# Weight loads cut into twelve pieces and a reordered attention-out chain in a one-core transformer block

## The chip, the cores and the metric

The kernel runs on one core of one Trainium2 chip. The metric is the device time of one execution in microseconds; the median over runs is quoted, and lower is better. The kernel before takes 227.86 us (median of three runs, 227.57 to 228.95). "Same" means within 2%.

Times inside a profile are microseconds from the start of its span. A span is 1.7 to 1.8 us shorter than the time of the same run (229.42 us with a span of 227.7 before).

## The reference

One block on x of shape [1, 2048, 448] in bf16, without biases or learned norms:

```python
phi = lambda t: jnp.where(t > 0, t + 1, jnp.exp(t)) + 1e-6
# A: linear attention, 16 heads of 28
pq, pk = phi(q), phi(k)                       # q, k, v from layernorm(x) @ wqkv
kv  = jnp.einsum("bhsd,bhse->bhde", pk, v)    # sums over ALL 2048 tokens
z   = jnp.einsum("bhsd->bhd", pk)
num = jnp.einsum("bhqd,bhde->bhqe", pq, kv)
den = jnp.einsum("bhqd,bhd->bhq", pq, z)[..., None] + 1e-6
h   = x + (num / den merged over heads) @ wo
# B: GeGLU, hidden width 1792
n   = layernorm(h)
h2  = h + (gelu_tanh(n @ w_gate) * (n @ w_up)) @ w_down
```

What matters: kv and z need every token, so there is a hard boundary. No attention output exists before the last of 16 token tiles (128 tokens each) has gone into kv, and the MLP of a tile needs that tile's attention output. Three MLP weights of 1,568 KB each must be on chip by then.

One thing about correctness: with weights of these scales the MLP's output is tiny beside h (an estimate from the reference's scales puts it below the rounding of h in bf16). So "correct" here vouches for the attention half, hardly for the MLP.

## The kernel before: the parts that matter

The kernel is a task graph. Every task names its engine, the buffers it reads and writes, a rough duration and a *key* (its rank; lower goes first). A list scheduler places the tasks on each engine in the order of its own model of time; the chip then runs these fixed orders, with semaphores for the dependences. The scheduler knows two modes of TensorE, 128 rows (everything except gate and up) and 64 rows (gate in partitions 0 to 63 and up in 64 to 127, side by side: in the trace of before the first gate and the first up matmul both start at 85.04 us). The choice of mode:

```python
if e == "pe":
    cur = [t for t in av if t.mode == pe_mode]
    oth = [t for t in av if t.mode != pe_mode]
    if cur and oth:
        rc = min(max(f, t.ready) for t in cur)
        ro = min(max(f, t.ready) for t in oth)
        hyst = MODE_HYST_64 if pe_mode == 64 else MODE_HYST_128
        av = cur if rc <= ro + hyst else oth      # stays in its mode while it has work
```

Stage 1 normalises x and transposes it. The first four tiles are transposed on TensorE, the other twelve by DMA, issued from SyncE ("SPq" in the profile):

```python
# ... for each tile t: statistics, rstd, xn = normalised x ...
if t < N_PE_TR:        # 4
    # four TensorE transposes, evicted by VectorE
else:
    G.add("sp", lambda e: e.dma_start_transpose(xnT[:, :, tok], xn[:, sl, :]),
          name="xT%d" % t, key=t - 3.0, ...)
```

For each pair of tiles, TensorE then forms K and V from xnT, ScalarE takes exp of K ("ek") and copies V, GpSimd and VectorE finish phi, and TensorE accumulates kv ("acc"). The three MLP weights are one load each, issued from ScalarE's queue ("ACTq") once the last tile of x is there:

```python
big = [b_x[15]]
dma(wgu_sb[0:64, :, :],   B_w_gate.rearrange("(k p) n -> p k n", p=64),  [b_wg], "dwg", ..., q="act", key=8.0, r=big)
dma(wgu_sb[64:128, :, :], B_w_up.rearrange("(k p) n -> p k n", p=64),    [b_wu], "dwu", ..., q="act", key=8.0, r=big)
dma(wd_sb[:, :, :],       B_w_down.rearrange("(j p) n -> p j n", p=128), [b_wd], "dwd", ..., q="act", key=8.0, r=big)
```

The attention-out chain of a tile, `a2_tile(t)`, uses one set of PSUM banks (4, 5, 6) for all tiles:

```python
ka = K_A2 + 0.01 * t if t < 4 else K_Q + 0.04 * (t - 3) + 0.005     # K_A2 = 15.5, K_Q = 17.0
# nd:   psND(bank 4)  = pq^T kvz                           TensorE
# rd, om: o = num * reciprocal(den)                        VectorE
# tro:  transpose o into bank 6 (TensorE), evicted by ScalarE   [t < 2; later tiles by DMA]
# wo:   psH(bank 5)   = o @ wo                             TensorE
# hr:   h = psH + x, statistics, rstd (ScalarE log/exp for t < 2), norm
# trh:  transpose of norm(h) into bank 6 (TensorE), evicted by ScalarE   [t < 2; later by DMA]
```

Its Q groups (16 of them; matmul, exp, clamp, phi) have keys from 17.0. The table of the gelu is preloaded after all exp work. Gate and up then run in chunks of 2, 2, 4, 4, 4 tiles (`gu_chunk`) and down follows tile by tile.

## Time and profile before

The stages, as read from the TensorE timeline ("first K of tile 4" is the first matmul that needs a DMA transpose):

| milestone, us | before |
|---|---|
| first K matmul | 8.18 |
| first K of tile 4 | 31.79 |
| end of the last kv accumulation | 62.53 |
| first gate/up matmul | 85.04 |
| end of span | 227.7 |

The next lines are the profile page of the kernel before, parts 1 and 2: busy time per engine, and the span in 40 slices of 5.7 us. A digit is the busy share in tenths; PEclk is TensorE's granted clock in tenths; the last row is what the DMA engines moved.

```profile
PE 200.5 (88%) x1666; PEld 114.1 (50%) x1666; DVE 124.1 (55%) x320; ACT 75.2 (33%) x193; POOL 54.5 (24%) x121
...
PE   6790039999996769999998999999999999999995
...
PEclk9798556999999779999999999999999999999999
DMA  7969999400001226300166500044520003000011
GB/s 220 322 169 206 213 269 239 94 4 1 0 0 26 46 45 90 60 0 4 46 122 137 96 3 1 3 104 107 105 40 0 3 21 79 23 0 3 1 40 40
```

TensorE is the bound (88%), with a hole in slices 4 to 6 and a weak stretch in slices 13 to 15, each with a lower clock. In the hole the DMA engines are full (9) and move only 206 to 269 GB/s.

The view of stage windows of the kernel before. Columns: window, its length, busy time (and instructions) of the five engines, mean granted clock, DMA share, GB/s.

```profile
8.18:31.79 23.61, 9.36 (x55) 4.14 (x53) 13.03 (x43) 7.46 (x24) 7.81 (x15) 0.72 1.00 210
31.79:62.53 30.74, 30.33 (x185) 15.25 (x186) 12.26 (x24) 13.86 (x30) 14.13 (x25) 0.89 0.42 90
62.53:85.04 22.51, 17.28 (x104) 9.06 (x102) 17.92 (x42) 14.28 (x22) 7.81 (x14) 0.87 0.14 27
85.04:227.70 142.66, 138.83 (x1281) 81.38 (x1280) 76.02 (x197) 37.32 (x113) 22.58 (x52) 1.00 0.22 46
```

In the first window TensorE works 9.4 of 23.6 us; in the third 17.3 of 22.5, part of it at half clock (75.8 to 79.2 us and from 82.6 us on, by the clock records of this trace). The second and the last are nearly full.

The TensorE timeline of the kernel before, around the hole (start, length, instruction, idle time before it and what ended it), and then its table of waits (total, times, longest):

```profile
17.11 0.42 PE L514 MATMUL ps<-v,pk 128*113 128x113 bf16 x4
31.79 1.30 PE L477 MATMUL ps<-wkv_sb,xnT 128*128 128x448 bf16 x3 [14.25 <-DMA xnT<-xn]
33.49 1.30 PE L477 MATMUL ps<-wkv_sb,xnT 128*128 128x448 bf16 x3 [0.41 <-DMA xnT<-xn]
```

```profile
PE ps L477 <- DMA xnT<-xn: 14.7, 2, 14.3
...
PE ps L666 <- DMA hnT<-hn: 1.0, 1, 1.0
```

DMA issues of the kernel before (the last column is the median time from issue to landing), and the view of the xnT tile, which gives that time as minimum, median and maximum over the twelve transposes:

```profile
wgu_sb<-in_B_w_gate_dram ACTq DMA_DIRECT2D x1, 1568.0 KB, 10.4
wgu_sb<-in_B_w_up_dram ACTq DMA_DIRECT2D x1, 1568.0 KB, 17.9
wd_sb<-in_B_w_down_dram ACTq DMA_DIRECT2D x1, 1568.0 KB, 24.3
```

```profile
DMA to landing us min/median/max: 2.4/7.2/17.4
```

A transpose takes 2.4 us when nothing is in its way and up to 17.4 us beside the weights. That is the hole.

ScalarE's timeline of the kernel before, between the last kv accumulation and the first gate/up matmul (other instructions left out), shows four loads of activation tables:

```profile
72.38 1.28 ACT L618 ACT_TABLE_LOAD   x1
...
75.70 1.28 ACT L424 ACT_TABLE_LOAD   x1
...
79.67 1.28 ACT L426 ACT_TABLE_LOAD   x1
...
84.20 1.28 ACT L690 ACT_TABLE_LOAD   x1
```

### The profile page before, as it was taken

To read this page: it belongs to the slowest core of one execution; us is meant where nothing else is said; L and a number is where in the kernel's file an instruction comes from. 1 tells how busy PE (TensorE), PEld (TensorE's weight loads), DVE (VectorE), ACT (ScalarE), POOL (GpSimd) and SP (SyncE) were. 2 spreads that over 40 slices of the span, in tenths; PEclk is the share of its full clock that TensorE was granted. 3 is DMA by queue.
4 is the path that set the end of the run, shared out by engine and by line. 5 is a ranking of instruction groups with operands and counts; after the bars stand their busy time and mean duration, and the time that the engine had idled before them with its cause. 6 is when DMAs were issued, how large, how long until landed. Compare 5 with 4: busy or idle time off the path is not lost.

```text
span 227.7 us, 4477 instructions
## 1 busy us (share of the span) xinstructions
PE 200.5 (88%) x1666; PEld 114.1 (50%) x1666; DVE 124.1 (55%) x320; ACT 75.2 (33%) x193; POOL 54.5 (24%) x121
## 2 busy tenths in 40 slices
PE   6790039999996769999998999999999999999995
PEld 6340004455553338898554555555455554455552
DVE  4988010634599576454877545676654452454422
ACT  3265003465467463344000443300244400344300
POOL 3066024624455036000354100054400030000000
PEclk9798556999999779999999999999999999999999
DMA  7969999400001226300166500044520003000011
GB/s 220 322 169 206 213 269 239 94 4 1 0 0 26 46 45 90 60 0 4 46 122 137 96 3 1 3 104 107 105 40 0 3 21 79 23 0 3 1 40 40
DMA packets 37637, 17.00 MB, mean 75 GB/s; under 512 B 29488, under 2 KB 36720, under 8 KB 37616
## 3 DMA queue, kind: packets, MB, share of 16 engines
q1 hardware_dynamic: 34400, 11.50, 24.0%
q10 hardware_dynamic: 3216, 5.22, 9.6%
q8 instruction: 13, 0.21, 0.4%
q14 instruction: 8, 0.07, 0.1%
HBM read 8.26 MB, written 1.84 MB: 44 GB/s over the span
## 4 chain that ended last, share of the span: by engine, by line
PE 76%; DMA 10%; DVE 8%; ACT 3%; issue 1%; POOL 1%; SPq 0%; DVEq 0%; ACTq 0%
PE ps L666 34%; PE ps L629 18%; DMA xnT<-xn 7%; PE ps L583 5%; PE ps L668 4%; PE ps L485 4%; PE ps L477 4%; PE ps L539 3%; DVE st L414 2%; DVE pqT L544 2%; PE ps L488 2%; PE ps L514 2%; DMA x_sb<-in_A_x_dram 1%; DMA hnT<-hn 1%; DVE x_sb L586 1%
## 5 line engine op out<-in xcount | busy, mean ns | idle before, releaser
L666 PE MATMUL ps<-hnT,wgu_sb 64*128 64x512 bf16 (+1 forms) x490 | 86.0, 335 | 1.0 <-DMA hnT<-hn 1.0
L668 PE MATMUL ps<-hnT,wgu_sb 64*128 64x512 bf16 (+1 forms) x490 | 86.1, 335 | 0.0
L690 ACT ACTIVATE gl<-ps 128x256 bf16<-128x256 f32 x112 | 36.9, 381 | 92.6 <-PE ps L668 57.3
L692 DVE TENSOR_TENSOR hh<-ps,gl 128x256 bf16<-128x256 f32 x112 | 42.3, 420 | 43.0 <-ACT gl L690 43.0
L666 PEld LDWEIGHTS ps<-hnT,wgu_sb 64*128 64x128 bf16 x490 | 46.0, 94 | 27.9 <-issue 2.1
L668 PEld LDWEIGHTS ps<-hnT,wgu_sb 64*128 64x128 bf16 x490 | 42.6, 94 | 4.9 <-DVE hh L692 1.4
L629 PE MATMUL ps<-wd_sb,hh 128*128 128x448 bf16 x224 | 44.0, 352 | 0.0
L629 PEld LDWEIGHTS ps<-wd_sb,hh 128*128 128x128 bf16 x224 | 21.5, 98 | 19.5 <-issue 0.4
L419 POOL TENSOR_SCALAR nm<-mv 128x1 f32<-128x1 f32 (+1 forms) x20 | 4.6, 233 | 92.5 <-DVE mv L415 84.5
L477 PE MATMUL ps<-wkv_sb,xnT 128*128 128x448 bf16 x48 | 13.0, 409 | 14.7 <-DMA xnT<-xn 14.7
L633 DVE TENSOR_TENSOR x_sb<-ps,x_sb 128x448 bf16<-128x448 f32 x16 | 10.0, 625 | 19.7 <-PE ps L629 19.7
L414 DVE BATCH_NORM_STATS2 st<-x_sb 128x6 f32<-128x448 bf16 x32 | 19.4, 609 | 1.6 <-DMA x_sb<-in_A_x_dram 1.5
L583 PE MATMUL ps<-wo_sb,oT 128*128 128x448 bf16 x64 | 16.8, 390 | 1.5 <-DVE x_sb L586 0.8
L539 PE MATMUL ps<-xnT,wq_sb 128*113 128x512 bf16 x64 | 16.3, 382 | 0.6 <-DVE pqT L544 0.5
L508 ACT ACTIVATE v<-ps 128x448 bf16<-128x448 f32 x16 | 7.9, 542 | 24.4 <-PE ps L489 24.4
L506 DVE SCALAR_TENSOR_TENSOR pk<-ps,tm 128x448 bf16<-128x448 f32 x16 | 9.3, 616 | 12.1 <-POOL tm L504 12.1
L477 PEld LDWEIGHTS ps<-wkv_sb,xnT 128*128 128x128 bf16 x48 | 4.6, 109 | 19.3 <-DMA xnT<-xn 15.6
L453 DVE COPY xn<-xn 128x64 bf16<-128x64 bf16 x16 | 4.1, 259 | 15.1 <-POOL xn L451 15.0
L504 POOL TENSOR_SCALAR tm<-e 128x448 bf16<-128x448 bf16 x16 | 8.7, 561 | 14.2 <-ACT e L503 12.4
L485 PE MATMUL ps<-wkv_sb,xnT 128*128 128x448 bf16 x48 | 12.0, 387 | 0.0
L586 DVE TENSOR_TENSOR x_sb<-ps,x_sb 128x448 bf16<-128x448 f32 x16 | 9.9, 621 | 3.7 <-PE ps L583 2.6
L451 POOL TENSOR_SCALAR xn<-x_sb,nm,rs 128x448 bf16<-128x448 bf16 x12 | 8.6, 720 | 13.7 <-DMA xnT<-xn 13.6
(63 smaller groups left out, 173.4 us busy)
## 6 DMA issues: line engine op xcount, KB each, us to landing
out_dram<-x_sb SPq DMA_DIRECT2D x16, 112.0 KB, 1.7
wgu_sb<-in_B_w_gate_dram ACTq DMA_DIRECT2D x1, 1568.0 KB, 10.4
wgu_sb<-in_B_w_up_dram ACTq DMA_DIRECT2D x1, 1568.0 KB, 17.9
wd_sb<-in_B_w_down_dram ACTq DMA_DIRECT2D x1, 1568.0 KB, 24.3
x_sb<-in_A_x_dram SPq DMA_DIRECT2D x3, 448.0 KB, 5.4
wkv_sb<-in_A_wqkv_dram ACTq DMA_DIRECT2D x1, 336.0 KB, 3.3
wkv_sb<-in_A_wqkv_dram SPq DMA_DIRECT2D x1, 336.0 KB, 4.1
wq_sb<-in_A_wqkv_dram SPq DMA_DIRECT2D x3, 112.0 KB, 6.1
```

Of the source, the lines that this page charges most:

```text
L414: op("dve", lambda e: e.bn_stats(st[:, t, :], src_ap), [b_src], [b_st[t]], "bnst%d" % t, 0.53, key)
L477: ins = e.matmul(ps[:, BK_K[t % 4], 0:D], xnT[:, k, t * 128:(t + 1) * 128], wkv_sb[:, k, 0:D], start=(k == 0), stop=False)
L485: ins = e.matmul(ps[:, BK_V[t % 2], 0:D], xnT[:, k, t * 128:(t + 1) * 128], wkv_sb[:, k, D:2 * D], start=(k == 0), stop=False)
L539: ins = e.matmul(psQ, wq_sb[:, k, g, 1:GP + 1], xnT[:, k, c * QCH:(c + 1) * QCH], start=(k == 0), stop=(k == 3))
L583: ins = e.matmul(psH, oT[:, so, g, :], wo_sb[:, g, :], start=(g == 0), stop=(g == 3))
L586: op("dve", lambda e, t=t, psH=psH: e.tensor_tensor(h_sb[:, t, :], psH, x_sb[:, t, :], ALU.add), bank(BK_H) + [b_x[t]], [b_h[t]], "hr%d" % ...
L629: ins = e.matmul(psO, hh[:, j, (t % HR) * 128:(t % HR + 1) * 128], wd_sb[:, j, :], start=(j == 0), stop=(j == NJ - 1))
L633: op("dve", lambda e, t=t, psO=psO: e.tensor_tensor(x_sb[:, t, :], psO, h_sb[:, t, :], ALU.add), bank(bk) + [b_h[t]], [b_x[t]], "out%d" % ...
L666: e.matmul(psG[:, jj * N:(jj + 1) * N], wgu_sb[A_, k, j * 128:(j + 1) * 128], hnT[A_, ka_, c0:c0 + N], start=(k == 0), stop=(k == 6))
L668: ins = e.matmul(psU[:, jj * N:(jj + 1) * N], wgu_sb[B_, k, j * 128:(j + 1) * 128], hnT[B_, kb_, c0:c0 + N], start=(k == 0), stop=(k == 6))
L690: G.add("act", lambda e, gi=gi, cs_=cs_, psG=psG: e.activation(gl[:, gi, cs_], psG[:, cs_], AF.Gelu_apprx_tanh), r=bank(BK_G[i]), w=[b_glh ...
L692: op("dve", lambda e, dst=dst, srcU=srcU, srcL=srcL: e.tensor_tensor(dst, srcU, srcL, ALU.mult), bank(BK_U[i]) + [b_glh], [b_ar[j_][t % HR ...
```

## The change

The intent is to close both holes: to let the first transposes through by loading the weights a little at a time, and to run the first two tiles' attention-out chains beside each other, first in rank, so that gate and up can start earlier. There are four parts.

1. **Pieces.** Twelve pieces (each weight in four column blocks, rows of 768 to 1,024 bytes for gate and up), each issued from ScalarE's queue right after the K exp of tiles 1 to 12.
2. **Lockstep.** The chain of tiles 0 and 1 becomes a generator that yields between its four steps, and both advance together; each has banks of its own; their rank is −60, ahead of everything; the gelu table is preloaded after them; the ranks of the later tiles are reshuffled.
3. **Mode rule.** After 2.5 us in 64-row mode, ready 128-row work of a better rank may break in. This spreads the remaining attention-out tiles into the first gate/up chunks.
4. **x tile 1** is loaded first on the other queue.

```diff
+MODE_MIN_64 = 2.5
@@ schedule
-                        av = cur if rc <= ro + hyst else oth
+                        if pe_mode == 64 and ro <= rc and rc - mode_since >= MODE_MIN_64 and min(t.key for t in oth if t.ready <= max(f, ro)) < min(t.key for t in cur):
+                            av = oth
+                        else:
+                            av = cur if rc <= ro + hyst else oth
@@ loads
+        JS = [(0, 4), (4, 7), (7, 11), (11, 14)]        # column blocks of 128
+        def big_piece(n, key, after):
+            p_ = n // 2 if n < 8 else n - 8
+            a_, c_ = JS[p_]
+            cs = slice(a_ * 128, c_ * 128)
+            if n >= 8:
+                dma(wd_sb[:, a_:c_, :], B_w_down[cs, :].rearrange("(j p) n -> p j n", p=128), ..., q="act", after=[after])
+            elif n % 2 == 0:
+                dma(wgu_sb[0:64, :, cs], B_w_gate[:, cs].rearrange("(k p) n -> p k n", p=64), ..., q="act", after=[after])
+            else:
+                dma(wgu_sb[64:128, :, cs], B_w_up[:, cs].rearrange("(k p) n -> p k n", p=64), ..., q="act", after=[after])
         dma(x_sb[:, 0:1, :], xv[:, 0:1, :], b_x[0:1], "dx0", 128 * D * 2)
+        dma(x_sb[:, 1:2, :], xv[:, 1:2, :], b_x[1:2], "dx1", 128 * D * 2, q="act")
-        dma(x_sb[:, 1:2, :], xv[:, 1:2, :], b_x[1:2], "dx1", 128 * D * 2)
-        big = [b_x[15]]
-        dma(wgu_sb[0:64, :, :], B_w_gate..., "dwg", ...)      # and dwu, dwd: the three bulk loads
@@ after each K exp
-                act_exp(... "ek%d" % t ...)
+                ek = act_exp(... "ek%d" % t ...)
+                if 0 <= t - T_W < 12:                   # T_W = 1
+                    big_piece(t - T_W, kk, ek)
@@ a2_tile
-            ka = K_A2 + 0.01 * t if t < 4 else K_Q + 0.04 * (t - 3) + 0.005
+            ka = K_A2 + 0.0 * t if t < N_FIRST else K_A2R + 0.04 * t      # K_A2 = -60, N_FIRST = 2, K_A2R = 17.2
+            bnd, bto, bh, bth = FIRST_BK[t] if t < N_PE_A2 else (BK_ND, None, BK_H, None)   # ((4,6,6,6),(5,7,7,7))
+            yield                                       # after om, after tro, after the statistics
@@ main loop
-                a2_tile(done); done += 1
+                grp = [a2_tile(t) for t in range(done, done + (N_PE_A2 if done == 0 else 1))]
+                done += len(grp)
+                for _ in range(4):
+                    for gen in grp:
+                        next(gen, None)
+            if t0 == 0:
+                tbl2 = G.add("act", ... preload gelu table ...)
```

(Cut: the Q groups' banks go from 7, 0, 1, 2, 3 to 0, 1, 2, 3, and the readers of the weights wait for the piece they need.)

More of the change, by code (lines that the diff above doesn't have):

```diff
@@ L101, in schedule @@
         pe_mode = 128
+        mode_since = 0.0
         while left:
@@ L132, in schedule @@
             if e == "pe":
+                if t.mode != pe_mode:
+                    mode_since = st
                 pe_mode = t.mode
@@ L241, in bass_sequential_preLN__linear_attn_block__glu_gated_geglu__prompt_kernel @@
     WARM = cfg.get("warm", 40)
+    T_W = cfg.get("t_w", 1)
     LN_LEAD = cfg.get("ln_lead", 4.0)
-    K_A2 = cfg.get("k_a2", 15.5)
+    K_A2 = cfg.get("k_a2", -60.0)
+    K_A2R = cfg.get("k_a2r", 17.2)
+    N_FIRST = cfg.get("n_first", 2)
     K_Q = cfg.get("k_q", 17.0)
@@ L312, in bass_sequential_preLN__linear_attn_block__glu_gated_geglu__prompt_kernel @@
         b_wk, b_wv, b_wq = bufs("wk", 2), bufs("wv", 2), bufs("wq", 4)
-        b_wo, b_wd = bufs("wo", 3), _Buf("wd")
-        b_wg, b_wu = _Buf("wg"), _Buf("wu")
+        b_wo = bufs("wo", 3)
+        JS = [(0, 4), (4, 7), (7, 11), (11, 14)]
+        j2p = [p_ for p_, (a_, c_) in enumerate(JS) for _ in range(a_, c_)]
+        b_wg, b_wu, b_wd = bufs("wg", 4), bufs("wu", 4), bufs("wd", 4)
         b_ident, b_ones, b_mask2, b_mask3, b_mtmp, b_mones = (_Buf(n) for n in ("ident", "ones", "mask2", "mask3", "mtmp", "mones"))
@@ L335, in bass_sequential_preLN__linear_attn_block__glu_gated_geglu__prompt_kernel @@
         BK_Q0 = cfg.get("bk_q0", (7,))
-        BK_Q = cfg.get("bk_q", (7, 0, 1, 2, 3))
-        BK_T2 = 6
+        BK_Q = cfg.get("bk_q", (0, 1, 2, 3))
+        FIRST_BK = ((4, 6, 6, 6), (5, 7, 7, 7))
         BK_ND, BK_H = 4, 5
@@ L344, in bass_sequential_preLN__linear_attn_block__glu_gated_geglu__prompt_kernel, with dma @@
         ik = [-300.0]
-        def dma(out_ap, in_ap, w, name, nbytes, q="sp", key=None, r=()):
+        def dma(out_ap, in_ap, w, name, nbytes, q="sp", key=None, r=(), after=()):
             ik[0] += 0.01
-            return G.add(q, lambda e: e.dma_start(out_ap, in_ap), r=r, w=w, name=name, kind="dma", key=ik[0] if key is None else key, nbytes=nbytes)
+            return G.add(q, lambda e: e.dma_start(out_ap, in_ap), r=r, w=w, name=name, kind="dma", key=ik[0] if key is None else key, nbytes=nbytes, after=after)
+        def big_piece(n, key, after):
+            p_ = n // 2 if n < 8 else n - 8
+            a_, c_ = JS[p_]
+            cs = slice(a_ * 128, c_ * 128)
+            nb = (c_ - a_) * 128 * D * 2
+            if n >= 8:
+                dma(wd_sb[:, a_:c_, :], B_w_down[cs, :].rearrange("(j p) n -> p j n", p=128), [b_wd[p_]], "dwd%d" % p_, nb, q="act", key=key, after=[after])
+            elif n % 2 == 0:
+                dma(wgu_sb[0:64, :, cs], B_w_gate[:, cs].rearrange("(k p) n -> p k n", p=64), [b_wg[p_]], "dwg%d" % p_, nb, q="act", key=key, after=[after])
+            else:
+                dma(wgu_sb[64:128, :, cs], B_w_up[:, cs].rearrange("(k p) n -> p k n", p=64), [b_wu[p_]], "dwu%d" % p_, nb, q="act", key=key, after=[after])
         def op(eng, fn, r, w, name, dur, key=None, lat=None):
@@ L373, in bass_sequential_preLN__linear_attn_block__glu_gated_geglu__prompt_kernel @@
         dma(wo_sb[0:64, 3, :], A_wo[384:448, :], [b_wo[1]], "dwo_t", 64 * D * 2)
-        big = [b_x[15]]
-        dma(wgu_sb[0:64, :, :], B_w_gate.rearrange("(k p) n -> p k n", p=64), [b_wg], "dwg", D * FF * 2, q="act", key=8.0, r=big)
-        dma(wgu_sb[64:128, :, :], B_w_up.rearrange("(k p) n -> p k n", p=64), [b_wu], "dwu", D * FF * 2, q="act", key=8.0, r=big)
-        dma(wd_sb[:, :, :], B_w_down.rearrange("(j p) n -> p j n", p=128), [b_wd], "dwd", FF * D * 2, q="act", key=8.0, r=big)
         op("pool", lambda e: e.memset(ones_bf[:], 1.0), [], [b_ones], "ones", 0.20)
@@ L502, in bass_sequential_preLN__linear_attn_block__glu_gated_geglu__prompt_kernel @@
                 psK3 = psK.rearrange("p (g e) -> p g e", g=NG)
-                act_exp(lambda e, ie=ie, psK=psK: e.activation(e1[:, ie, :], psK, AF.Exp), bank(BK_K[t % 4]), [b_e1[ie]], "ek%d" % t, _c_act(D), kk)
+                ek = act_exp(lambda e, ie=ie, psK=psK: e.activation(e1[:, ie, :], psK, AF.Exp), bank(BK_K[t % 4]), [b_e1[ie]], "ek%d" % t, _c_act(D), kk)
+                if 0 <= t - T_W < 12:
+                    big_piece(t - T_W, kk, ek)
                 op("pool", lambda e, ie=ie: e.tensor_scalar(tm1[:, ie, :], e1[:, ie, :], 1.0 + EPS, 0.0, ALU.min, ALU.max),
@@ L549, in a2_tile @@
             c = t // 4
-            ka = K_A2 + 0.01 * t if t < 4 else K_Q + 0.04 * (t - 3) + 0.005
-            psND = ps[:, BK_ND, 0:NG * 116]
+            ka = K_A2 + 0.0 * t if t < N_FIRST else K_A2R + 0.04 * t
+            bnd, bto, bh, bth = FIRST_BK[t] if t < N_PE_A2 else (BK_ND, None, BK_H, None)
+            psND = ps[:, bnd, 0:NG * 116]
             nd3 = psND.rearrange("p (a b) -> p a b", b=29)
@@ L559, in fnnd @@
                 return ins
-            G.add("pe", fnnd, r=[b_pqT[g][c] for g in range(NG)] + [b_kvz, b_kvz2], w=bank(BK_ND), name="nd%d" % t, dur=_c_mm(116, 4), lat=PE_L, key=ka)
-            op("dve", lambda e, i=i, nd3=nd3: e.reciprocal(rd[:, i, :], nd3[:, :, 28]), bank(BK_ND), [b_rd[i]], "rd%d" % t, 0.17, ka)
+            G.add("pe", fnnd, r=[b_pqT[g][c] for g in range(NG)] + [b_kvz, b_kvz2], w=bank(bnd), name="nd%d" % t, dur=_c_mm(116, 4), lat=PE_L, key=ka)
+            op("dve", lambda e, i=i, nd3=nd3: e.reciprocal(rd[:, i, :], nd3[:, :, 28]), bank(bnd), [b_rd[i]], "rd%d" % t, 0.17, ka)
             op("dve", lambda e, i=i, so=so, nd3=nd3: e.tensor_tensor(o_sb[:, so, 0:D].rearrange("p (a e) -> p a e", e=28), nd3[:, :, 0:28],
                                                                rd[:, i, :].unsqueeze(2).to_broadcast([128, 16, 28]), ALU.mult),
-               bank(BK_ND) + [b_rd[i]], [b_o[so]], "om%d" % t, 0.54, ka)
+               bank(bnd) + [b_rd[i]], [b_o[so]], "om%d" % t, 0.54, ka)
+            yield
             if t < N_PE_A2:
-                tvo = psb[:, BK_T2, 0:512].rearrange("p (k t) -> p k t", k=4)
+                tvo = psb[:, bto, 0:512].rearrange("p (k t) -> p k t", k=4)
                 def ftro(e, so=so, tvo=tvo):
@@ L572, in ftro @@
                     return ins
-                G.add("pe", ftro, r=[b_o[so], b_ident], w=bank(BK_T2), name="tro%d" % t, dur=_c_mm(128, 4), lat=PE_L, key=ka)
-                op("act", lambda e, so=so, tvo=tvo: e.activation(oT[:, so, :, :], tvo, AF.Identity), bank(BK_T2), [b_oT[so]], "evo%d" % t, _c_act(512), ka)
+                G.add("pe", ftro, r=[b_o[so], b_ident], w=bank(bto), name="tro%d" % t, dur=_c_mm(128, 4), lat=PE_L, key=ka)
+                op("act", lambda e, so=so, tvo=tvo: e.activation(oT[:, so, :, :], tvo, AF.Identity), bank(bto), [b_oT[so]], "evo%d" % t, _c_act(512), ka)
             else:
@@ L577, in a2_tile @@
                   name="oT%d" % t, kind="dmat", dur=1.25, lat=1.3, key=ka)
-            psH = ps[:, BK_H, 0:D]
+            yield
+            psH = ps[:, bh, 0:D]
             def fnwo(e, so=so, psH=psH):
@@ L584, in fnwo @@
                 return ins
-            G.add("pe", fnwo, r=[b_oT[so]] + b_wo, w=bank(BK_H), name="wo%d" % t, dur=_c_mm(D, 4), lat=PE_L, key=ka)
-            op("dve", lambda e, t=t, psH=psH: e.tensor_tensor(h_sb[:, t, :], psH, x_sb[:, t, :], ALU.add), bank(BK_H) + [b_x[t]], [b_h[t]],
+            G.add("pe", fnwo, r=[b_oT[so]] + b_wo, w=bank(bh), name="wo%d" % t, dur=_c_mm(D, 4), lat=PE_L, key=ka)
+            op("dve", lambda e, t=t, psH=psH: e.tensor_tensor(h_sb[:, t, :], psH, x_sb[:, t, :], ALU.add), bank(bh) + [b_x[t]], [b_h[t]],
                "hr%d" % t, 0.54, ka)
@@ L594, in a2_tile @@
                 ln_rstd_pool(t, mv2, ln2, rs2, b_mv2, b_ln2, b_rs2, ka)
+            yield
             sh = t % HN_R
@@ L603, in a2_tile @@
             if t < N_PE_A2:
-                tvh = psb[:, BK_T2, 0:896].rearrange("p (k t) -> p k t", k=7)
+                tvh = psb[:, bth, 0:896].rearrange("p (k t) -> p k t", k=7)
                 def ftrh(e, sh=sh, tvh=tvh):
@@ L610, in ftrh @@
                     return ins
-                G.add("pe", ftrh, r=[b_hn[sh], b_hnd[sh], b_ident], w=bank(BK_T2), name="trh%d" % t, dur=_c_mm(128, 7), lat=PE_L, key=ka)
-                op("act", lambda e, t=t, tvh=tvh: e.activation(hnT[:, :, (t % HR) * 128:(t % HR + 1) * 128], tvh, AF.Identity), bank(BK_T2), [b_hnT[t % HR]],
+                G.add("pe", ftrh, r=[b_hn[sh], b_hnd[sh], b_ident], w=bank(bth), name="trh%d" % t, dur=_c_mm(128, 7), lat=PE_L, key=ka)
+                op("act", lambda e, t=t, tvh=tvh: e.activation(hnT[:, :, (t % HR) * 128:(t % HR + 1) * 128], tvh, AF.Identity), bank(bth), [b_hnT[t % HR]],
                    "evh%d" % t, _c_act(896), ka)
@@ L616, in a2_tile @@
                   name="hT%d" % t, kind="dmat", dur=1.6, lat=1.3, key=ka)
-        tbl2 = G.add("act", lambda e: e.preload_act_table(AF.Gelu_apprx_tanh), name="tbl2", dur=1.3, key=K_B1 - 1.0, kind="nosync", after=exp_tasks)
         def b2_tile(t, split):
@@ L630, in fnd @@
                 return ins
-            G.add("pe", fnd, r=[(b_ar[j][t % HR], j if j >= split else 0) for j in range(NJ)] + [b_wd], w=bank(bk), name="down%d" % t,
+            G.add("pe", fnd, r=[(b_ar[j][t % HR], j if j >= split else 0) for j in range(NJ)] + [(b_wd[j2p[j]], j) for j in range(NJ)], w=bank(bk), name="down%d" % t,
                   dur=_c_mm(D, NJ), lat=PE_L, key=kd, mw=True)
@@ L670, in fngu @@
                     return ins
-                G.add("pe", fngu, r=[b_hnT[t % HR] for t in tiles] + [b_wg, (b_wu, 1)], w=[(b_ps[BK_G[i]], 0), (b_ps[BK_U[i]], 1)], name="gu%d" % v,
+                G.add("pe", fngu, r=[b_hnT[t % HR] for t in tiles] + [(b_wg[j2p[j0 + jj]], 14 * jj) for jj in range(nj)] + [(b_wu[j2p[j0 + jj]], 14 * jj + 1) for jj in range(nj)], w=[(b_ps[BK_G[i]], 0), (b_ps[BK_U[i]], 1)], name="gu%d" % v,
                       dur=_c_mm(N, 7 * nj), lat=PE_L, key=kb, mode=64, mw=True)
@@ L702, in bass_sequential_preLN__linear_attn_block__glu_gated_geglu__prompt_kernel @@
             while done < min(T, t0 + HR):
-                a2_tile(done)
-                done += 1
+                grp = [a2_tile(t) for t in range(done, done + (N_PE_A2 if done == 0 else 1))]
[4 more added lines that the diff above has]
+            if t0 == 0:
+                tbl2 = G.add("act", lambda e: e.preload_act_table(AF.Gelu_apprx_tanh), name="tbl2", dur=1.3, key=K_B1 - 1.0, kind="nosync", after=exp_tasks)
             gu_chunk(t0, nt)
```

## The prediction

> **What bounds the kernel now.** TensorE is busy 200.5 of 227.7 us (busy table). Its timeline shows two places of lost time.
> (a) From 17.5 to 31.8 us it is idle, and the next K group is split until 33.5: the wait table gives 14.7 us for the K matmul on the DMA transpose of xn. Three weight loads, issued at 13.0 to 14.4 us on the other queue, land after 10.4, 17.9 and 24.3 us (DMA issues); the first three transposes, issued at 15.0 to 17.8, land 17 us later, the last ones after 2.4. The gap also halves the granted clock (0.50 from 22 to 38 us in the windows): about 2.3 us more. [...] Gate and up have one packet per 3,584-byte row[...]; the DMA engines are full while moving only about 210 GB/s.
> (b) From the last KV accumulation (62.5) to the first gate/up matmul (85.0) there are 22.5 us, with about 12.5 us of TensorE work at full clock. The chain there walks serially through two tiles sharing banks 4, 5, 6, with DVE serving Q work in between, three extra 1.28 us table loads (ScalarE returns to log/exp for tile 1), and half clock at about 75 to 86 us.

> **What the change does.**
> 1. Weights in 12 pieces of 768 to 1,024-byte rows (wd's stay 896), one after each K exp. The first transposes meet one piece. Estimate: the gap of 16 us falls to about 1; the clock stays at 1.0, 2.3 us; contention in the K stage gives back 2 to 3 us, because two pieces (estimated 3.6 us of DMA) and two transposes (1.8 us) exceed the 4.2 us of a pair of tiles. Net -15. Twelve issues cost ScalarE's sequencer 0.6 us each; there is room.
> 2. Lockstep, own banks, first rank, one table load. Estimated chain: kvz 1.3, nd/rd/om to 3.5, transpose and eviction to 4.6, wo 5.6, residual and statistics 7.8, norm 8.6, transpose and two evictions (0.92 each) 10.5 us; but the queued Q groups, nine after the last accumulation instead of seven, must also run: about 12.3 us on TensorE, 11.5 on ScalarE. I expect 15 us instead of 22.5; work moved across the boundary cancels. Net -7.
> 3. The mode rule puts the remaining attention-out tiles into the first gate/up chunks: about 18 more 64/128-row switches at 0.1 us (+1.8), DVE nearly full there (about 4.0 us per 4.05 of TensorE), +1.5; the hnT wait near 123 us disappears, -1.2.
> 4. x tile 1 first on the other queue: -0.5.

> Sum: -15 -7 +1.8 +1.5 -1.2 -0.5 = about -20.5.

> **Predicted: 207 us, 8 in 10 within 200 to 214.** Faster by over 2%: 0.96; within 2%: 0.03; slower: 0.01.

> **Signs.** Right: first transposes land within 5 us; K waits for them under 4 us in total; clock near 1.0 from 14 us on; last accumulation near 47 us; first gate/up matmul near 62; one table load between; no hnT wait.
> Wrong: transposes over 7 us while pieces move; ScalarE held by piece issues; TensorE waiting on hh or oT over 3 us in the first gate/up chunks.

> **What would break it.** Pieces to 64 partitions could move no faster than 210 GB/s and keep transposes late in every pair (+5). DVE order could stall TensorE in the mixed stage (+4).

The six terms make −20.4 (the text says about −20.5), and 227.86 less that is about 207.

Beside three of the small figures, what the traces show:

- A mode switch, 0.1 us in the scheduler's model: on the critical chain of before, the first gate/up matmul after 128-row work takes 0.32 us and the next ones 0.21 (from 160.15 us on), and the first wo group after gate/up 0.86 us and the next one 0.76 (at 145.03 and 148.75 us).
- An issue, 0.6 us: the three weight issues of before held ScalarE's sequencer for 0.59 to 0.65 us.
- Two transposes, 1.8 us: the 512 packets of one take 0.8 us in before when the weights are through (42.7 to 43.4 and 44.0 to 44.7 us), and 0.8 to 0.9 us for tiles 4 to 6 in after.

## The result and the profile after

The changed kernel takes **215.66 us** (median of four runs, 214.05 to 215.72). Before took 228.41 in these rounds (227.57 to 229.08). The ratio is 0.942 (95% interval 0.938 to 0.947): faster. The outputs are right. Here and below a ratio is the mean time of one kernel's fast runs over that of the other's in the same rounds, so it is not quite the ratio of the medians quoted beside it. The gain is 12.75 us by medians where about 20.9 were predicted, and 215.66 lies above the predicted range of 200 to 214.

One caution for the two profiles: that of before comes from a slow run (229.42 us with a span of 227.7), that of after from its fastest (214.05 with 212.3). The difference of spans, 15.4 us, overstates the gain.

| milestone, us | before | predicted | after |
|---|---|---|---|
| first K matmul | 8.18 | about 7.7 | 7.68 |
| first K of tile 4 | 31.79 | | 17.09 |
| end of the last kv accumulation | 62.53 | near 47 | 49.99 |
| first gate/up matmul | 85.04 | near 62 | 65.48 |
| end of span | 227.7 | | 212.3 |

The page of the changed kernel, parts 1 and 2 (a slice is now 5.3 us):

```profile
PE 198.1 (93%) x1666; PEld 113.1 (53%) x1666; DVE 123.2 (58%) x320; ACT 70.8 (33%) x190; POOL 54.5 (26%) x121
...
PE   8688399998977999999999999999999999999994
...
PEclk9999979999997999999999999999999999999999
DMA  6987999920102244485554000461000001000011
GB/s 199 348 202 162 179 211 191 299 72 0 22 6 49 46 91 74 90 120 108 75 106 76 22 2 3 76 139 44 6 0 3 0 29 47 14 0 5 0 43 43
```

The hole has shrunk to one slice (the "3"), but PEclk still shows two dips, and the DMA engines are full for slices 5 to 8. The same stages by windows:

```profile
7.68:17.09 9.41, 8.21 (x55) 3.74 (x52) 9.41 (x32) 4.79 (x16) 5.04 (x10) 1.00 0.92 227
17.09:49.99 32.90, 28.10 (x177) 14.25 (x178) 16.06 (x39) 16.69 (x41) 16.91 (x31) 0.95 0.91 177
49.99:65.48 15.49, 12.78 (x91) 7.94 (x90) 14.68 (x34) 10.25 (x19) 6.85 (x13) 1.00 0.05 10
65.48:212.30 146.82, 144.08 (x1302) 82.53 (x1300) 78.86 (x205) 37.06 (x112) 23.56 (x54) 0.99 0.25 47
```

The first stage lost 14.2 us and the third 7.0 us, as intended. The second grew by 2.2 us although TensorE has less to do in it (28.1 us busy against 30.3): it idles 4.8 us there, and the clock averages 0.95. The last grew by 4.2 us.

The TensorE timeline of the changed kernel where the second stage loses its time:

```profile
17.09 0.74 PE L496 MATMUL ps<-wkv_sb,xnT 128*128 128x448 bf16 x3 [0.36 <-DMA xnT<-xn]
...
22.60 0.73 PE L496 MATMUL ps<-wkv_sb,xnT 128*128 128x448 bf16 x3 [1.53 <-ACT v L529]
25.50 1.23 PE L496 MATMUL ps<-wkv_sb,xnT 128*128 128x448 bf16 x3 [2.17 <-DMA xnT<-xn]
...
26.90 1.92 PE L560 MATMUL ps<-xnT,wq_sb 128*113 128x512 bf16 x4
```

Tile 6's K waits 1.53 us and tile 7's 2.17 us. Then the same instructions take nearly twice as long: a Q group 1.92 us instead of 1.03, because the clock is at half from 25.6 to 29.0 us. The first of the two waits is put down to ScalarE's copy of V; but the transpose of tile 6 lands at about 22.4 us, just before the matmul starts at 22.60, so a DMA is at least as good a reading there. The transposes of tiles 4 to 7, issued at 14.3, 15.6, 16.9 and 18.3 us, land after 2.8, 2.5, 5.5 and 7.1 us. The view of the tile, and the table of waits:

```profile
DMA to landing us min/median/max: 2.5/6.4/8.2
```

```profile
PE ps L496 <- DMA xnT<-xn: 2.8, 3, 2.2
PE ps L580 <- DVE o_sb L584: 1.9, 1, 1.9
...
PE ps L496 <- ACT v L529: 1.5, 1, 1.5
```

The worst case fell from 17.4 to 8.2 us, but the median hardly moved (7.2 to 6.4). In place of the hnT wait of before there is none. The wait on o_sb is a new one; it stands just before the first gate/up matmul in the timeline of the changed kernel:

```profile
61.34 0.56 PE L634 MATMUL ps<-ident,hn 128*128 128x128 bf16 x7
62.69 0.56 PE L634 MATMUL ps<-ident,hn 128*128 128x128 bf16 x7 [0.79 <-DVE hn L627]
65.17 0.38 PE L580 MATMUL ps<-kvz,pqT 113*128 113x116 bf16 x4 [1.91 <-DVE o_sb L584]
65.48 0.28 PE L690 MATMUL ps<-hnT,wgu_sb 64*128 64x256 bf16 x1
```

From 66.5 to 70.0 us the clock is at half again. ScalarE's timeline has one table load in this stage instead of four:

```profile
61.77 1.28 ACT L733 ACT_TABLE_LOAD   x1
```

The packet records of the two traces say more about the transposes (read from the records by queue; SPq carries the transposes, ACTq the weights):

```
before  gate packets 14.4 to 22.0   up 22.0 to 30.4   down 29.7 to 36.6
        transpose of tile 4: issued 15.0, no packet recorded before 22.2;
        its 512 packets of 256 B (22.2 to 30.6) run beside up's 448
after   piece 0 lands by about 16.6; transpose of tile 6: data 18.1 to 19.0, completion only 20.5 to 21.3
        piece 1 packets 18.8 to 21.2; piece 2 20.6 to 23.6
        transpose of tile 7: issued 18.3, first packet 22.1; tiles 8 and 9: 23.6 to 25.7
        piece 3: issued 21.3, first packet 25.6
```

### The profile page after: what moved, and what is told of

Same layout as the page of the kernel before. It is cut to its first block, busy times and chain, and to the rows that moved or that the text cites. A ratio compares the mean times of both kernels' runs of the same rounds, so it can differ in the third digit from the quotient of the medians.

```text
span 212.3 us, 4508 instructions
## 1 busy us (share of the span) xinstructions
PE 198.1 (93%) x1666; PEld 113.1 (53%) x1666; DVE 123.2 (58%) x320; ACT 70.8 (33%) x190; POOL 54.5 (26%) x121
## 3 DMA queue, kind: packets, MB, share of 16 engines
q10 hardware_dynamic: 6192, 5.33, 10.5%
## 4 chain that ended last, share of the span: by engine, by line
PE 83%; DVE 9%; DMA 5%; ACT 1%; issue 1%; POOL 0%; DVEq 0%; POOLq 0%; ACTq 0%
PE ps L690 34%; PE ps L653 20%; PE ps L692 8%; PE ps L607 6%; PE ps L560 5%; DVE st L433 3%; DMA xnT<-xn 3%; PE ps L504 3%; PE ps L496 3%; PE ps L580 2%; PE ps L535 2%; DMA x_sb<-in_A_x_dram 1%; PE ps L507 1%; DVE pqT L565 1%; DVE pk L527 1%
## 5 line engine op out<-in xcount | busy, mean ns | idle before, releaser
L692 PE MATMUL ps<-hnT,wgu_sb 64*128 64x512 bf16 (+1 forms) x490 | 89.0, 339 | 0.0
L690 PE MATMUL ps<-hnT,wgu_sb 64*128 64x512 bf16 (+1 forms) x490 | 88.7, 338 | 0.0
L653 PEld LDWEIGHTS ps<-wd_sb,hh 128*128 128x128 bf16 x224 | 21.5, 98 | 20.5 <-issue 1.3
L657 DVE TENSOR_TENSOR x_sb<-ps,x_sb 128x448 bf16<-128x448 f32 x16 | 10.0, 624 | 23.4 <-PE ps L653 23.4
L496 PE MATMUL ps<-wkv_sb,xnT 128*128 128x448 bf16 x48 | 11.4, 365 | 4.4 <-DMA xnT<-xn 2.8
L607 PE MATMUL ps<-wo_sb,oT 128*128 128x448 bf16 x64 | 14.6, 354 | 0.0
L625 POOL TENSOR_SCALAR hn<-x_sb,nm,rs 128x448 bf16<-128x448 bf16 x14 | 10.0, 716 | 16.9 <-DMA hnT<-hn 15.5
L525 POOL TENSOR_SCALAR tm<-e 128x448 bf16<-128x448 bf16 x16 | 8.8, 562 | 19.0 <-ACT e L522 18.3
L563 ACT ACTIVATE e<-ps 113x512 bf16<-113x512 f32 x16 | 9.5, 600 | 12.2 <-PE ps L560 12.2
L564 POOL TENSOR_SCALAR tm<-e 113x512 bf16<-113x512 bf16 x16 | 9.8, 614 | 7.7 <-ACT e L563 6.0
L565 DVE SCALAR_TENSOR_TENSOR pqT<-ps,tm 113x512 bf16<-113x512 f32 x16 | 10.6, 678 | 1.4 <-POOL tm L564 1.4
L504 PE MATMUL ps<-wkv_sb,xnT 128*128 128x448 bf16 x48 | 10.7, 357 | 0.0
```

The lines of the kernel that those rows point to most:

```text
L496: ins = e.matmul(ps[:, BK_K[t % 4], 0:D], xnT[:, k, t * 128:(t + 1) * 128], wkv_sb[:, k, 0:D], start=(k == 0), stop=False)
L504: ins = e.matmul(ps[:, BK_V[t % 2], 0:D], xnT[:, k, t * 128:(t + 1) * 128], wkv_sb[:, k, D:2 * D], start=(k == 0), stop=False)
L565: op("dve", lambda e, i=i, c=c, g=g, psQ=psQ: e.scalar_tensor_tensor(pqT[:, g, c * QCH:(c + 1) * QCH], psQ, EPS, tm2[:, i, :], ALU.max, AL ...
L607: ins = e.matmul(psH, oT[:, so, g, :], wo_sb[:, g, :], start=(g == 0), stop=(g == 3))
L653: ins = e.matmul(psO, hh[:, j, (t % HR) * 128:(t % HR + 1) * 128], wd_sb[:, j, :], start=(j == 0), stop=(j == NJ - 1))
L690: e.matmul(psG[:, jj * N:(jj + 1) * N], wgu_sb[A_, k, j * 128:(j + 1) * 128], hnT[A_, ka_, c0:c0 + N], start=(k == 0), stop=(k == 6))
```

## The experiments

All runs below come with the kernel before. The unchanged kernel after the change was run again as a0, and e1, e2 and e3 shared its chip. "Stage 2" is from the first K of tile 4 to the last kv accumulation, "stage 3" from there to the first gate/up matmul, "stage 4" the rest. Full clock is first granted at anything between 4.0 and 13.2 us of the span in different profiles, and stage 2 of the changed kernel and its variants begins at anything between 16.70 us (e10) and 19.53 us (a0), but for e7, where the hole is back; so stages are compared by their lengths. Where a profile is of a slow run, this is said (a0, e3, e4).

**Theory A**: a weight piece, whatever its rows, still holds up the transposes behind it in stage 2; this, with the half clock that the waits cause, is what the prediction missed. There are three rivals. *Row length*: what the transposes pay goes with the length of the rows beside them, as the prediction assumed. *ScalarE*: the pieces cost through its sequencer, which issues them between its K exps. *Mode rule*: the loss is in the last stage. In the texts the letter A stands for theory A, and another letter for the rival that the run in question is set against.

### a0: the change again

No edit.

> The changed kernel itself, unedited, as the reference for the other runs on the same chip and to see how much one profile differs from the next (its first profile was of its fastest run, 212.3 us; three other runs were 213.9 to 214.0). Expected 214 to 216 us, with the waits of K for the transposes of tiles 6 and 7 of about 1.5 and 2.2 us each as in the first profile.

Measured: 214.84 us (214.58 to 218.97), before 228.08, ratio 0.940 (0.935 to 0.944). The profiled execution was a slow one (218.97), with full clock granted only at 13.2 us and a half-clock window twice as long (26.9 to 33.7). Its transposes land after 2.4/6.0/9.5 us (minimum/median/maximum) and stage 2 takes 34.1 us. The gain repeats, and so does the late landing.

### e1_late: all pieces later, still from ScalarE

```diff
+        # after scheduling: move the twelve issues behind the K exps of tiles 10 to 15, two each
+        after = "ek%d" % (10 + i // 2)
```

> Only the place of the 12 weight pieces in ScalarE's queue is changed: two after each K exp from tile 10 on, instead of one after each from tile 1 on; the order of all other work on every engine is the same. Theory A (the missing 5 us are the transposes of xn held up by weight pieces in the DMA engines: 5.5 to 8.2 us to landing instead of 2.5, then the half clock after the stall): all transposes land within 3.5 us, TensorE waits for none of them over 0.7 us, the clock stays 1.0, the last KV accumulation ends near 45 us instead of 50, and the time falls by 4 to 6 us against a0. Theory B (the K stage is slowed by DVE, GpSimd and ScalarE work, the long landings only coincide): the accumulation still ends near 50 us, the time within 1 us of a0. If the pieces come too late for gate/up, TensorE waits for them at the first gate/up matmul instead.

Measured: 217.51 us (216.79 to 218.47), ratio 0.952 (0.947 to 0.957): 2.7 us *slower* than a0, although the transposes are free of the weights (2.4/2.4/4.4 us). The ScalarE timeline of this run shows what went wrong ("ACTq" lines are DMA issues on ScalarE's sequencer; their length is the time the issue held it):

```profile
41.15 2.67 ACTq L360 DMA_DIRECT2D wgu_sb<-in_B_w_up_dram  x1
...
45.01 1.85 ACTq L360 DMA_DIRECT2D wd_sb<-in_B_w_down_dram  x1
46.96 0.54 ACT L522 ACTIVATE e<-ps 128x448 bf16<-128x448 f32 x1 [1.68 <-POOL tm L525]
46.98 3.80 ACTq L360 DMA_DIRECT2D wd_sb<-in_B_w_down_dram  x2
```

and its TensorE timeline what followed:

```profile
46.76 0.42 PE L535 MATMUL ps<-v,pk 128*113 128x113 bf16 x4 [2.19 <-DVE pk L527]
...
52.89 1.07 PE L560 MATMUL ps<-xnT,wq_sb 128*113 128x512 bf16 x4 [1.81 <-ACT e L563]
```

With several pieces outstanding, single issues held ScalarE for up to 2.67 us (0.37 to 0.87 in the change, where they are spaced), and the exps behind them came late; two half-clock windows followed (47.3 to 50.7 and 54.1 to 57.5). So e1 frees the transposes but brings in the ScalarE rival's cost, which the change itself does not have. As a test of A by time it is inconclusive. It says that the pieces must also leave ScalarE: e4.

### e2_longrows: the same pieces with long rows

Gate and up are cut along k instead of along columns: rows of 3,584 bytes as in the kernel before, pieces of the same number. Gate/up must then wait for all pieces.

```diff
+        KS = [(0, 2), (2, 4), (4, 6), (6, 7)]
-                dma(wgu_sb[0:64, :, cs], B_w_gate[:, cs].rearrange("(k p) n -> p k n", p=64), ...)
+                dma(wgu_sb[0:64, k0:k1, :], B_w_gate[k0 * 64:k1 * 64, :].rearrange("(k p) n -> p k n", p=64), ...)
```

(Two brackets are cut from the text below: the mechanism of the row-length rival, and a count of packets per engine that the records do not give.)

> The same number of pieces at the same places and nearly the same bytes each, but gate and up are cut by contraction blocks, so that every row is 3,584 bytes [...] instead of 768 to 1,024. If the row length is what helps [...], the transposes land later again and the time rises by 3 us or more against a0. If it is the size of the whole transfer that counts, landings and time are those of a0 within 1 us.

Measured: 216.74 us (215.51 to 217.63), ratio 0.947 (0.940 to 0.953), against 214.84 and 0.940 of a0; transposes 2.4/7.8/11.3 us. Row length is worth 0.7% by ratio or 1.9 us by medians, with intervals that overlap. Neither expected outcome came exactly: long rows hurt a little, far less than the row-length rival says. Most of the first gain does not come from the short rows.

### e3_spread: the same row length over 128 partitions

Gate and up rows 0 to 383 go to all 128 partitions, three k-blocks each, and the rest is added at the end in two more loads, so each of these pieces is also a seventh smaller. The layout is wrong for the matmuls (see the reference section on why this still compared as correct); bytes and their timing are what is tested.

```diff
-                dma(wgu_sb[0:64, :, cs],  B_w_gate[:, cs].rearrange("(k p) n -> p k n", p=64), ...)
+                dma(wgu_sb[:, 0:3, cs],   B_w_gate[0:384, cs].rearrange("(k p) n -> p k n", p=128), ...)
-                dma(wgu_sb[64:128, :, cs], B_w_up[:, cs].rearrange("(k p) n -> p k n", p=64), ...)
+                dma(wgu_sb[:, 3:6, cs],    B_w_up[0:384, cs].rearrange("(k p) n -> p k n", p=128), ...)
+            if n == 11:    # rows 384 to 447 of both
```

> Wrong result on purpose. The gate and up pieces have the same rows and bytes, but are laid over all 128 partitions instead of 64 (6 of 7 contraction blocks; the last blocks come in two transfers at the end), while the matmuls read what they read before. Theory C (a piece into 64 partitions moves at only about 215 GB/s, and the long time it holds the DMA engines is what keeps the transposes): a piece takes about 1.2 us instead of 2.1, the transposes of tiles 6 to 9 land 1 to 3 us earlier, and the time falls by 1.5 to 3 us against a0. If a transpose is held for a reason that has nothing to do with how long a piece takes, the time is that of a0 within 1 us.

Measured: 212.82 us (211.70 to 216.59), ratio 0.930 (0.924 to 0.935): 2.0 us below a0. The profile is of a slow run (216.59), as a0's is. Transposes 2.4/4.2/7.6; tile 6's lands later than in a0 (7.6 us against 5.5), tile 9's earlier (6.6 against 9.5), so the expected 1 to 3 us for tiles 6 to 9 came only in part. Stage 2 takes 32.6 us (34.1 in a0). In the packet records of e3 a 384-KB piece that runs nearly alone takes 1.1 us (the first one 1.7), where a 448-KB piece to 64 partitions takes mostly 2.0 to 2.6 us, which is about 180 to 230 GB/s (the 1,568-KB gate load of before: 211). The down pieces (128 partitions) reach 350 to 380 GB/s (in the trace of after, the windows of 1 us from 39 to 42 us, when they move, show 332 to 380). How long a piece holds the engines matters, while ScalarE's sequencer is held as long as in the change (7.3 us for all fourteen issues against 7.2 for twelve); that speaks for theory A and against the ScalarE rival.

### e4_sp: pieces on SyncE's queue, behind the last transpose

Same twelve pieces, same order on TensorE, VectorE and GpSimd, and on ScalarE minus the issues.

```diff
+        # after scheduling
+        for pc in pieces:
+            act.remove(pc)
+        at = [n for n, t in enumerate(sp) if t.name == "xT15"][0] + 1
+        sp[at:at] = pieces
```

> The 12 weight pieces are moved out of ScalarE's queue to the queue of the transposes, right after the last of the 12 transposes of xn; the order of all other work on every engine stays that of the changed kernel. Nothing then competes with a transpose, and ScalarE issues no weights. The run before this one that moved the pieces late left them on ScalarE, where its profile shows K exps and Q exps waiting 2.2 and 1.8 us around four issues in a row, so it settled nothing. Theory A (what is missing of the predicted gain is lost to pieces and transposes meeting, and to the half clock that the stall brings): transposes land in about 2.5 us, from the first K matmul of tile 4 to the end of the last KV accumulation it takes about 28 us instead of 32.9, the time is 4 to 6 us below the changed kernel, so about 209 to 211. Theory B (engine order in the K stage): 32 to 34 us for that stage and 214 to 216 us in all. If the weights come too late, TensorE waits for them at the first gate/up matmul or the first down matmul.

Measured: 210.95 us (207.82 to 212.34; six runs), before 228.69. The ratio of fast runs, 0.917 (0.908 to 0.927), rests on two runs, because one run at 207.82 makes the four at 210.95 and above count as slow. By medians the ratio is 0.922, against 0.942 of a0: 4 to 4.5 us of gain. The profile of this kernel (of its slowest run, 212.34), by the view of the tile and the window of stage 2:

```profile
DMA to landing us min/median/max: 2.4/2.5/4.4
```

```profile
18.30:47.03 28.73, 26.26 (x177) 13.50 (x178) 16.63 (x39) 16.86 (x41) 17.02 (x32) 1.00 0.80 158
```

Stage 2 takes 28.73 us instead of 32.90. Of the 4.2 us, 2.3 are TensorE's idle time (32.90 − 28.10 = 4.80 against 28.73 − 26.26 = 2.47) and 1.8 are the same work at a full clock (28.10 against 26.26 us busy). In a0's profile, with two windows' worth of half clock, the difference is 5.4 us. e8 has the same placing, and its profile, of a fast run, gives 28.73 us as well. Theory A is shown in its effect: with the pieces out of the transposes' way, their landing and stage 2 are what the prediction assumed (end of the last accumulation at 47.03, predicted near 47). By itself e4 also takes twelve issues off ScalarE; that this is not the cause is argued from e3, which kept every issue and still gained, and from the changed kernel's short issues.

The six runs contain a second finding: the run of 207.82 us had a mean granted clock of 1.000, the five others 0.983 to 0.984. The half-clock stretch (6.8 us in the profile) is worth 3 us here. Where it comes from is e8's subject.

### e5_nomode: the change without the mode rule

```diff
-MODE_MIN_64 = 2.5
+MODE_MIN_64 = 1e9
```

> Only the new rule that lets 128-row work break into the 64-row gate/up blocks is switched off (the minimum time in a block is set beyond the run); everything else is the changed kernel. The prediction put the mixing at +1.8 us of switches and +1.5 of DVE stalls against 1.2 us saved in the hnT wait: so the time should fall by about 2 us here. If mixing pays for itself (the attention-out chain of tiles 4 to 7 off the path), the time rises, and a wait for hnT near the third gate/up block comes back.

Measured: 217.61 us (216.74 to 218.32), ratio 0.953 (0.948 to 0.958): 2.8 us *slower* than a0. The expectation fell, and the mode-rule rival with it. The table of waits of this run shows the waits that the rule takes away:

```profile
PE ps L690 <- DMA hnT<-hn: 1.7, 2, 1.4
PE ps L607 <- DMA oT<-o_sb: 1.1, 1, 1.1
```

and after them a half-clock window at 110.3 to 113.7 us. The mode rule pays for its switches.

### e6_pieces: the pieces alone

The kernel before with only part 1 of the change.

```diff
-        dma(... the three bulk loads ...)
+                if 0 <= t - 1 < 12:
+                    big_piece(t - 1, kk, ek)
```

> The kernel before with the 12 pieces alone (weights one after each K exp from tile 1 on; banks, ranks, order of attention-out, table load, mode rule and the place of x tile 1 as before). The two profiles give from the last KV accumulation on 165.2 us before and 162.3 after, so most of the gain should be the pieces': expected ratio to before about 0.955 (218 us). If lockstep gives more than 4 us of its own, the ratio here is 0.965 or higher.

Measured: 218.56 us (217.84 to 218.91), before 228.69, ratio 0.957 (0.951 to 0.963): −10.1 us. The prediction gave this part −15. Transposes 2.4/5.9/8.6, as in the whole change.

### e7_lockstep: everything except the pieces

The changed kernel with the three bulk loads put back.

```diff
+        dma(... the three bulk loads, as in the kernel before ...)
-                if 0 <= t - T_W < 12:
-                    big_piece(t - T_W, kk, ek)
```

> The changed kernel with the three bulk loads of before in place of the pieces. The stall of K on the transposes is back: the first K matmul of tile 4 at about 31 us. Lockstep alone then gives what the two profiles show from the last accumulation to the end, 165.2 against 162.3 us, some 3 us, plus 0.5 from x tile 1: expected ratio to before 0.98 to 0.99 (224 to 225 us). If the parts overlap (attention-out is only short once the Q groups are not late), it gives less than 1 us.

Measured: 223.97 us (223.53 to 224.49), ratio 0.981 (0.975 to 0.987): −4.7 us, faster clear of the noise, but whether by more than 2% is unclear. The prediction's other terms sum to −7 + 1.8 + 1.5 − 1.2 − 0.5 = −5.4. Its stage 3 is 15.5 us. The two parts add: 0.957 + 0.981 − 1 = 0.938, beside 0.940 and 0.942 of the whole.

### e8_warm: e4 with TensorE kept busy before gate/up

In e4 as in the change, TensorE idles 0.79 and 1.91 us just before the first gate/up matmul, and a half-clock window follows (61.6 to 68.4 in e4's profile). Here 14 and 34 dummy matmuls into a bank that is free fill those two gaps. ("It" in the text below is this half clock. A sentence is cut from that text: it said that all profiles with this idle time show the half clock, which e5's and e7's do not.)

```diff
+                for nm, cnt in (("dum0", 14), ("dum1", 34)):     # placed behind trh0 and trh1
+                            ins = e.matmul(ps[:, 1, 0:128], ident[:], ident[:], start=True, stop=True)
```

> The kernel of the run with the weights on the transposes' queue, plus 48 matmuls on the identity into a free bank (14 after the transpose of hn of tile 0, 34 after that of tile 1), where TensorE otherwise idles 0.8 and 1.9 us just before the first gate/up matmul. [...] If the idle time causes it, the first gate/up chunk starts at full clock and the time falls by 1.5 to 3 us against the run without them (0.917 of before, so about 0.907). If not, the time stays within 0.7 us.

Measured: 209.30 us (208.12 to 209.68; before 227.90), ratio 0.919 (0.915 to 0.924). By medians 0.918 against 0.922 of e4: 0.9 to 1.7 us. By fast runs there is no gain (0.919 against 0.917, the latter from two runs), e4 ran in another call, and e11, in the same call and without the fill, takes 209.51. So the expected 0.907 was missed, and what the fill is worth in time is unclear. What it does to the clock is not. The TensorE timeline of this run, then its window of the last stage:

```profile
58.58 0.95 PE L737 MATMUL ps<-ident 128*128 128x128 bf16 x14
...
59.93 2.06 PE L737 MATMUL ps<-ident 128*128 128x128 bf16 x34
...
62.32 0.28 PE L690 MATMUL ps<-hnT,wgu_sb 64*128 64x256 bf16 x1
```

```profile
62.32:207.50 145.18, 142.39 (x1302) 82.41 (x1300) 78.77 (x205) 37.03 (x112) 23.51 (x54) 1.00 0.27 48
```

The fill does not delay gate/up (stage 3 is 15.5 us as before), and the last stage shrinks from 147.89 us in e4's profile to 145.18 at a clock of 1.00. All six runs have a clock of 0.992 to 1.000, where five of e4's six had 0.983 or 0.984. So the two short gaps can trigger the window.

They need not. e7's profile has the same two gaps without any fill:

```profile
73.83 0.56 PE L637 MATMUL ps<-ident,hn 128*128 128x128 bf16 x7 [0.79 <-DVE hn L630]
76.31 0.38 PE L583 MATMUL ps<-kvz,pqT 113*128 113x116 bf16 x4 [1.92 <-DVE o_sb L587]
```

The length of a window shows in this case's traces: half-clock stretches are 3.4 us or a multiple (25.6 to 29.0, 66.5 to 70.0, 61.6 to 68.4). The gaps that bring them here are 0.8 and 1.9 us, shorter than one window: what it took was a window that was less than half busy; it need not be idle.

### e9_all: the best version

e8 with 60 warm-up matmuls at the start instead of 40, and tile 4's numerator matmul placed behind the second gate/up chunk.

```diff
-    WARM = cfg.get("warm", 40)
+    WARM = cfg.get("warm", 60)
+        # "nd4" moved behind "gu1"; dummies and pieces as in e8
```

> A version that puts the parts together: weights after the transposes on their queue, the 48 filling matmuls, the numerator matmul of tile 4 moved behind the second gate/up group (before, the first gate/up waited for it though it needs nothing of it), and 60 instead of 40 warming matmuls at the start. If the parts add up: 0.900 of before or lower, 204 to 206 us.

Measured: **208.34 us** (207.77 to 208.76), ratio 0.915 (0.911 to 0.920), the lowest median of all, and about 3% below the change (0.915 against 0.942). The expected 0.900, 204 to 206 us, was not reached, and the intervals of e4, e8 and e11 overlap with this one.

### e10_bulk_sp: three uncut loads on SyncE's queue

e4 with bulk loads in place of the pieces, still behind the last transpose.

```diff
+        dma(... the three bulk loads ...), moved to SyncE's queue behind "xT15"
-                    big_piece(t - T_W, kk, ek)
```

> Lockstep and all else of the change, but the three bulk loads of before with 3,584-byte rows for gate and up, uncut, placed after the last transpose of xn on the queue of the transposes. If what matters is only that no weight transfer is in flight while the transposes of xn run, cutting is worth nothing: the ratio is that of the 12 pieces at the same place, 0.917 within 0.5 per cent. If cutting and short rows help by themselves, it is 1 per cent or more slower; if the weights come too late uncut, TensorE waits at the first gate/up or down matmuls.

Measured: 211.56 us (209.20 to 212.42; before 227.90), ratio 0.927 (0.921 to 0.933), transposes 2.4/2.5/4.7. By medians it is 0.928 against e4's 0.922, by fast runs 0.927 against 0.917 (two runs); in microseconds that is 0.6 (between the medians) to 2.3, and the intervals overlap. So what cutting is worth once the loads stand behind the transposes is unclear, but small beside the whole gain (0.927 uncut at this place, 0.942 cut at the old one). The *place* of the loads is what counts.

### e11_start: e4 with longer warm-up at the start

```diff
-    WARM = cfg.get("warm", 40)
+    WARM = cfg.get("warm", 60)
```

> The kernel of the run with the weights on the transposes' queue, with 60 warming matmuls at the start instead of 40 and the same order otherwise. The profiles so far differ by up to 2.4 us before the first K matmul of tile 4, by when the full clock comes (4.0 to 13.2 us) and whether it is lost again at about 7.5 us. If the gap after the 40 warming matmuls is the cause, runs agree better and the median falls by 1 to 2 us against 0.917 of before. If it is only the phase of the clock's window, nothing changes.

Measured: 209.51 us (206.74 to 210.40), ratio 0.916 (0.908 to 0.923). The median is 1.4 us below e4's, but the spread did not get smaller (3.7 us against 4.5), and a half-clock window stands at 61.5 to 65.0 as it would. Unclear; its part in e9 is therefore unclear too.

## Why the prediction was wrong

**The step that failed is the size of the first term**: "contention in the K stage gives back 2 to 3 us, because two pieces (estimated 3.6 us of DMA) and two transposes (1.8 us) exceed the 4.2 us of a pair of tiles. Net -15." Alone, the pieces gave −10.1 us (e6). The hole did close (first stage 23.6 to 9.4 us), so that part was right; the give-back was sized too small. Taking e4's 26.26 us of TensorE work at full clock as the floor, stage 2 gives back 32.90 − 26.26 = 6.6 us in the changed kernel (7.8 in a0's slower profile), in place of 2 to 3. Of these, 4.2 us (5.4 in a0's) go when the pieces are out of the way (e4); the other 2.5 are idle time that remains in e4 as well and that the term had not counted. There are three reasons.

- *The model was a rate, the cost is a queue.* I had counted DMA time per pair of tiles and taken the excess as loss. What the landing times show is that from tile 6 on the transposes stand behind whole pieces: tile 6's data had moved by 19.0 us, but its completion came at 20.5 to 21.3, with the end of piece 1; tile 7's was issued at 18.3 and its first packet is recorded at 22.1, after piece 1 and in the midst of piece 2. A transpose of 2.4 us then takes 6.4 at the median. e4, e1 and e10 bring it back to 2.4 to 2.5 by order alone.
- *The pieces are slow as well.* To half of the partitions 448 KB take 2.0 to 2.6 us, and e3 shows 2.0 us of gain from spreading them. The sum had this speed in it (3.6 us for two pieces, 784 KB, is 223 GB/s), so the speed was not mis-sized. What it left out is that transposes come late in every pair; "What would break it" named that with +5, and that is what happened: the risk was seen and priced as a risk, not in the sum.
- *Waits far shorter than the big hole bring a half-clock window, when they fill more than half of one window of the clock's grid.* The window of 22.2 to 25.6 us, with the end of tile 6's wait and nearly all of tile 7's 2.17 us, was busy for only 0.24 of its length and was followed by half clock from 25.6 to 29.0 us, 1.8 us more of busy time than e4 needs. I had counted the clock's loss in the big hole and none for the small ones.

**The mechanism given for it was at best half right.** I had assumed that a transpose's small packets take turns with the weights' large ones, so that shorter rows let them through sooner. The trace of before does have one packet of 3,584 bytes per row of gate and up (448 for each), and alternation from 22.2 us on (512 small packets beside 448 large ones), but for the 7 us before it none: nothing of the transpose issued at 15.0 is recorded while gate's 7.6 us run (14.4 to 22.0). And e2, with rows as long as before, loses only 1.9 us. So cutting the loads hardly helps by its short rows; that it helps because the first transposes meet less in front of them fits all the runs. What decides which queue goes first stays open: piece 3, issued at 21.3, itself waited until the transposes of tiles 8 and 9 were through at 25.6, and in before the transpose of tile 4 passed the down load that had been issued before it. So it is not simply the order of issue.

**A second, smaller miss: the clock "stays at 1.0".** The gaps before the first gate/up matmul bring a half-clock window in most profiles, though not in e5's and e7's. e8 fills them and the last stage goes from 147.9 to 145.2 us in the profile, the length that it has in e7's without the half clock (145.17).

**What held.**
- Stage 3, predicted 15 us, measured 15.5; one table load instead of four; parts 2 to 4 together −4.7 measured (e7) for −5.4.
- The mode rule, taken as +2.1 us against before. The last stage grew by 4.2 us in the profile, by 2.5 in e8 where the clock is full. What I took for a price worth noting is a gain against leaving it out (e5: 2.8 us slower without).
- x tile 1: −0.5 predicted, first K matmul 8.18 to 7.68 in these two profiles; but a0 and e4, with the same order of loads, have 8.04, so the effect is not separated from the scatter of the start.
- Signs: no hnT wait, one table load, K waits for transposes, predicted under 4 us in total, 2.8 (4.3 with the 1.5 put down to ScalarE). First transposes within 5 us: true for tiles 4 and 5, not for 6 on. "Wrong" sign seen: transposes over 7 us while pieces move.

**The sum closes, nearly.** The shortfall is about 8 us. e4's placing gives back 4 to 4.5 us, e8's fill 0.9 to 1.7 us by medians (unclear by fast runs), and e8's milestones (46.83 and 62.32) are then those of the prediction. About 2 us are left. A slip of mine would account for most of them: I read the terms off a profile that belongs to a run of 229.42 us and took them from a median of 227.86, 1.6 us less. This last point is argued from the two numbers, not tested. How much of the run-to-run scatter comes from when the full clock is first granted is open too; e11 did not settle it.

## What to carry to other kernels

When bulk loads delay small transfers that an engine waits for (here transposes, 2.4 us to landing when undisturbed and up to 17.4 us beside the loads), look first at *what stands in front of* the small ones. Placing the bulk behind the last of them (here 4 to 4.5 us, with no change to the loads; it came with another queue, and the two were not separated) beat cutting it into pieces that still ran among them, and what the cutting was worth after that was lost in the noise (0.6 to 2.3 us). Check from which engine the bulk is issued, because an engine with work on the critical path can be held by a late issue (in e1 for up to 2.67 us, against 0.37 to 0.87 where the issues were spaced); and after every change look at the granted clock for half-speed windows: here one followed every window of 3.41 us in which TensorE was busy for less than half, so that gaps of one to two microseconds were enough when they fell into the same window. Dummy work can fill them (e8: a clock of 0.992 to 1.000 in six of six runs); whether that pays in time e8 leaves unclear.
